# Output items of a pair of batches in neighbouring row parities in turn, stored by one transfer with 4 KB rows; U two items behind V

## The chip, the cores and the metric

The kernel runs on one core of a Trainium2 chip. The core's engines work side by side, each with its own instruction stream: TensorE (PE; its weight loads are listed apart as PEld), VectorE (DVE), ScalarE (ACT), GpSimd (POOL), and SyncE (SP), which here only starts transfers. Sixteen transfer engines move data between the chip's memory (HBM) and the on-chip SBUF; TensorE writes its results into PSUM, eight banks of 2 KB in each of 128 partitions. The metric is the device time of one execution in microseconds (us); lower is better.

## The reference

Eight batches, eight heads, 576 positions, head size 64. Four heads attend to a local window of 32 positions, four to positions at a stride of 32. The heads' outputs, side by side, are x (8 x 576 x 512). The second half mixes x in the frequency domain and ends with a rectified product:

```python
scores = np.where(masks[None, :, :, :], scores, -1000000000.0)
attn = np.exp(scores - np.max(scores, axis=-1, keepdims=True))
attn = attn / (np.sum(attn, axis=-1, keepdims=True) + 1e-09)
x = np.matmul(attn, v)                       # then heads side by side: 8 x 576 x 512
X = np.fft.rfft(x, axis=1)                   # the first 64 modes are mixed
Yr = np.einsum('bmd,mde->bme', Xr, w_r) - np.einsum('bmd,mde->bme', Xi, w_i)
Yi = np.einsum('bmd,mde->bme', Xr, w_i) + np.einsum('bmd,mde->bme', Xi, w_r)
y = np.fft.irfft(Y, n=S, axis=1)             # the other modes are zero
u = x + y
return u + np.maximum(u @ w_ch, 0.0)         # 8 x 576 x 512, float32
```

## The kernel before

Most of the time goes to streaming the mode weights w_r and w_i (64 modes of two 512 x 512 matrices, f32 in HBM, f16 in SBUF) through queues that GpSimd starts, while attention, the forward transform and the products of each mode run under them. The spectrum Y (tile YT) grows mode by mode. In the second half of the run most of the inverse transform is folded in early: `renew` adds what the first three groups of sixteen modes give to the tiles v0 (which hold x @ w_ch, kept as "V") and xo (which hold x, kept as "U").

What is left at the end, and what the change is about, is the last group of modes and the output. The output is cut into 18 items (`items`, L973 to L976). An item is a set of batches and a row tile t. For t < 4 an item has two neighbouring batches and 128 of the 576 rows; tiles t and t+1 (t even) hold the even and the odd rows of the same 256 rows, so a partition's row in tile t and its row in tile t+1 are neighbours in HBM. The last two items (t = 4) hold four batches each and the last 64 rows.

Each item passes these steps:

- `v_early` (L987): two 128 x 512 matmuls with the identity put v0 into a PSUM pair (pool "p").
- `u_early` (L992): the same for xo, into a pair of pool "p" (even items) or "u" (odd items).
- `new_rows` (L1001): for each batch one matmul over only 32 partitions adds the last group of modes, to V from the tile zz (spectrum times w_ch) and to U from the tile yy (spectrum). Batch b uses the 32 partitions of group b mod 4. Matmuls over different groups can run in the array at the same time.
- `v_done` (L1013): ScalarE writes relu(V) into the SBUF tile rl.
- `u_done` (L1020): VectorE adds U and rl into an SBUF tile osb, and SyncE starts the store (L1028). Items with t = 4 are stored by four small transfers, from SyncE for even and ScalarE for odd batches (L1031).

PSUM pool "p" has three pairs, "u" one. osb comes from pool "pw", which has five buffers of 8 KB a partition, the same that held weights before. The rows of one item in one batch are 2 KB each in HBM, and neighbours of an item's rows belong to the other parity, so a store of an item moves runs of 2 KB.

The order of the items is: pair 0 and pair 1 of batches in turn for t = 0, then t = 1, and so on to 3; then pairs 2 and 3; then the two last items. The loop (L1065 to L1081) works on V of item k and U of item k-1 in the same turn, in this order on TensorE: v_early(k), u_early(k-1), new_rows of V(k), new_rows of U(k-1). Ahead of it, V of items 0 and 1 and U of item 0 are put into PSUM under the last modes (`late[22]`), and after the last spectrum the rows of V0 and V1, then U0 and U1, are finished. At item 8 the second half of the last spectrum is multiplied with w_ch (`spec_z(3, 1, held)`), because items from there on belong to batches 4 to 7. The kernel fixes the order of each engine's instructions itself; an engine runs them in order and waits on semaphores.

Of the kernel before, what the change touches and what calls it, by code (L numbers as in the profile page):

```python
# [10 lines left out]
FP = mybir.dt.float32  # L11
F16 = mybir.dt.float16
AluOp = mybir.AluOpType
# [5 lines left out]
DM = 512  # L19
# [37 lines left out]
def kernel(  # L57
# [10 lines left out]
    nc = tc.nc  # L68
# [9 lines left out]
    def psum_pools(**bufs):  # L78
        pctx.close()
        pss.clear()  # L80
        for n, c in bufs.items():
            pss[n] = pctx.enter_context(
                tc.tile_pool(name="ps_" + n, bufs=c, space=PSUM)
            )

    def psum(kind, half=False, pair=False):
        if pair:
            return pss[kind].tile([128, 2, 512], FP, tag=kind, name=kind)
        if half:
            return pss[kind].tile([128, 1024], F16, tag=kind, name=kind)  # L90
        return pss[kind].tile([128, 512], FP, tag=kind, name=kind)
# [39 lines left out]
    pw = ctx.enter_context(tc.tile_pool(name="pw", bufs=NWBUF))  # L131
# [118 lines left out]
    def act_copy(out, in_):  # L250
        nc.scalar.activation(out=out, in_=in_, func=ACTF.Copy)  # L251
# [445 lines left out]
    def out_cols(t):  # L697
        if t < 4:
            return ds(256 * (t % 2) + 128 * (t // 2), 128)
        return ds(512, 64)  # L700
# [32 lines left out]
    def spec_z(g, bq, zp):  # L733
        for e in range(4):
            lhs = YS["YT"][:, e, g, ds(8 * bq, 8), :].rearrange("p x m -> p (x m)")
            nc.tensor.matmul(
                zp, lhs, w_chs["n"][:, e, :], start=(e == 0), stop=(e == 3)
            )
# [131 lines left out]
    yys = [ptr.tile([128, DM], F16, name=f"yy{i}") for i in range(B)]  # L870
# [96 lines left out]
    for n, i in enumerate([3, 5, 7] + list(range(8, 21))):  # L967
        b, t = n // 2, n % 2 * 2
# [3 lines left out]

    items = []  # L973
    for P0 in (0, 2):
        items += [((2 * P, 2 * P + 1), t) for t in range(4) for P in (P0, P0 + 1)]
    items += [(range(b, b + 4), 4) for b in (0, 4)]  # L976
    LAST = len(items) - 1
    vps, ups, rls, osbs = {}, {}, {}, {}

    def own(item, kept, half):  # L980
        bs, t = item
        return [kept[b][:, t] for b in bs] if t < 4 else [half[b // 2] for b in bs[::2]]

    def v_early(k):
        vps[k] = psum("p", pair=True)
        for j, r in enumerate(own(items[k], v0s, v0h)):
            nc.tensor.matmul(vps[k][:, j], idn, r, start=True, stop=False)  # L987

    def u_early(k):
        ups[k] = psum(("p", "u")[k % 2], pair=True)  # L990
        for j, r in enumerate(own(items[k], xos, xoh)):
            nc.tensor.matmul(ups[k][:, j], idn, r, start=True, stop=False)  # L992

    def new_rows(k, acc, spectra):
        bs, t = items[k]
        for j, b in enumerate(bs):
            q = ds(32 * (b % 4), 32)
            o, cols = acc[:, j % 2], out_cols(t)
            if t == 4:
                o = acc[ds(64 * (b % 2), 64), j // 2]  # L1000
            nc.tensor.matmul(  # L1001
                o, A3[q, cols], spectra[b // 4][q], start=False, stop=True
            )

    def pieces(k):
        return [slice(0, 1), slice(1, 2)] if k == 0 else [slice(0, 2)]

    def v_done(k):
        rl = ptr.tile([128, 2, 576], FP, tag=("xT", "rl")[k // 2 % 2], bufs=2, name="rl")
        rls[k] = rl[:, :, 0:DM]  # L1010
        vp = vps.pop(k)
        for j in pieces(k):
            nc.scalar.activation(out=rls[k][:, j], in_=vp[:, j], func=ACTF.Relu)  # L1013

    def u_done(k):
        bs, t = items[k]
        up, rl = ups.pop(k), rls.pop(k)
        osb = pw.tile([128, 2, DM], FP, tag="w", name="osb")
        for j in pieces(k):
            nc.vector.tensor_tensor(  # L1020
                out=osb[:, j], in0=up[:, j], in1=rl[:, j], op=AluOp.add
            )
            if t < 4:
                rows = out[:, ds(128 * (t - t % 2), 256), :].rearrange(
                    "b (p i) e -> p b i e", i=2
                )
                own_b = slice(bs[0] + j.start, bs[0] + j.stop)
                nc.sync.dma_start(rows[:, own_b, t % 2], osb[:, j])  # L1028
        if t == 4:
            for b in bs:  # L1030
                (nc.scalar if b % 2 else nc.sync).dma_start(  # L1031
                    out[b, ds(512, 64), :], osb[ds(64 * (b % 2), 64), b // 2 % 2, :]
                )
# [23 lines left out]
        new_rows(k, vps[k], zzs)  # L1057
    for k in range(2):
        v_done(k)
    for k in range(2):  # L1060
        if k:
            u_early(k)
        new_rows(k, ups[k], yys)
        u_done(k)
    for k in range(2, LAST + 2):  # L1065
        if k == 8:
            held = psum("p", pair=True)[:, 0]
            spec_z(3, 1, held)
            act_copy(zzs[1], held)
        if k <= LAST:  # L1070
            v_early(k)
        if k > 2:
            u_early(k - 1)
        if k <= LAST:
            new_rows(k, vps[k], zzs)
        if k > 2:
            new_rows(k - 1, ups[k - 1], yys)
        if k <= LAST:
            v_done(k)
        if k > 2:  # L1080
            u_done(k - 1)  # L1081
    psum_pools()


# [28 lines left out]
```

## Time and profile before

Device time, median of three runs: 427.61 us (427.32 to 427.89). The profiled execution has a span of 426.7 us from the first to the last instruction; the profile gives that span as its time, and the medians include 0.9 us more around it.

| what | value |
|---|---|
| span of the profiled execution | 426.7 us |
| median of three runs | 427.61 us |
| last weights used, spectrum complete | about 393.3 us |
| first and last add into osb start | 396.16 and 420.06 us |
| one add, 128 x 1024 | 1.225 us |
| one relu, 128 x 1024 | 1.02 us |
| stores by SyncE of 512 KB, issue to landing | 3.4 us median |
| start of one store's issue on SyncE | 0.37 us |
| mean granted TensorE clock | 0.926 |

How to read it: times are from the start of the span. A line of a timeline or a chain gives the start, the duration, the engine, the source line, the operation, the tile written and the tiles read. "SPq" and "ACTq" are instructions that these engines' sequencers run, such as starting a transfer. Landing is when the whole transfer has been signalled as done.

### The profile page before, as it was taken

What the parts mean: (1) busy time and instruction counts of PE and PEld (TensorE: products, weight loads), DVE (VectorE), ACT (ScalarE), POOL (GpSimd) and SP (SyncE); (2) the same over time, 40 slices, a digit from 0 to 9 for tenths busy, and PEclk for the clock granted to TensorE, in tenths of its full rate; (3) what the DMA queues carried; (4) which work ended last, traced back from release to release, by engine and by line L of the source; (5) the groups of instructions that cost most, each with busy time, mean ns of one, the idle gap of its engine ahead of it and who ended that gap; (6) DMA issues with size and microseconds to landing.
All of it is one profiled execution on the core that took longest, in us unless ns stands there. A gap on an engine that the chain in (4) does not pass through costs nothing.

```text
span 426.7 us, 9768 instructions
## 1 busy us (share of the span) xinstructions
PE 346.4 (81%) x4167; PEld 208.2 (49%) x4167; DVE 234.7 (55%) x466; ACT 218.3 (51%) x390; POOL 110.7 (26%) x196
## 2 busy tenths in 40 slices
PE   2977878769999698889768788878788867889993
PEld 2866767554656365566433344435444423445330
DVE  3788778851355154356113246746676354655884
ACT  1687678643656356556642235423442444443872
POOL 8332333322423222222222322222232222210000
PEclk9999899967999689999995889989999979989997
DMA  8999999999999999999999999999999999995698
GB/s 150 210 212 212 213 213 213 211 211 211 214 213 213 213 213 215 212 214 215 210 214 211 213 214 213 210 213 215 212 213 214 213 213 214 214 212 105 244 355 287
DMA packets 30938, 91.62 MB, mean 215 GB/s; under 512 B 4464, under 2 KB 5232, under 8 KB 30896
## 3 DMA queue, kind: packets, MB, share of 16 engines
q0 software_dynamic: 25168, 81.28, 96.2%
q1 hardware_dynamic: 4976, 9.13, 5.9%
q10 hardware_dynamic: 752, 0.61, 0.5%
q8 instruction: 32, 0.52, 0.5%
q14 instruction: 10, 0.08, 0.0%
HBM read 162.83 MB, written 9.44 MB: 404 GB/s over the span
## 4 chain that ended last, share of the span: by engine, by line
DMA 47%; PE 29%; DVE 14%; ACT 5%; issue 3%; DVEq 0%; POOL 0%; ACTq 0%; POOLq 0%
DMA wt<-in_moe_w_i_dram 38%; DMA wt<-in_moe_w_r_dram 7%; PE y L597 5%; DVE xb L241 3%; DVE kz L283 3%; PE p L987 2%; ACT X L251 2%; PE sc L532 2%; PE tp L413 2%; PE sc L459 1%; PE p L1001 1%; PE y L532 1%; PE p L760 1%; DVE yy L752 1%; DVE rec L240 1%
## 5 line engine op out<-in xcount | busy, mean ns | idle before, releaser
L597 PE MATMUL y<-wt,X 128*32 128x512 f16 (+1 forms) x448 | 70.9, 430 | 20.1 <-DMA wt<-in_moe_w_i_dram 20.1
L186 POOL DMA_DIRECT2D wt<-in_moe_w_r_dram x59 | 34.7, 588 | 126.4 <-PE y L597 56.3
L186 POOL DMA_DIRECT2D wt<-in_moe_w_i_dram x60 | 35.4, 590 | 68.3 <-DMA wt<-in_moe_w_i_dram 44.4
L597 PEld LDWEIGHTS <-X 128*32 128x32 f16 (+1 forms) x448 | 28.1, 140 | 39.4 <-DMA wt<-in_moe_w_i_dram 18.6
L727 DVE COPY xo<-tp 128x512 f16<-128x512 f16 x32 | 22.1, 691 | 36.8 <-PE tp L725 36.8
L726 ACT ACTIVATE v<-sc 128x512 f16<-128x512 f32 x32 | 19.1, 597 | 44.2 <-PE sc L717 44.2
L717 PE MATMUL sc<-w_cp,xT 128*128 128x512 f16 x128 | 36.9, 410 | 1.9 <-DVE xT L690 1.9
L489 ACT ACTIVATE PL<-sc 128x480 f16<-128x480 f32 (+1 forms) x48 | 27.0, 578 | 21.3 <-PE sc L475 21.0
L241 DVE TENSOR_TENSOR xb<-av,rec 90x256 f16<-90x256 f32 (+2 forms) x80 | 36.0, 450 | 2.8
L240 DVE RECIPROCAL rec<-av 90x4 f32<-90x4 f32 (+2 forms) x80 | 14.6, 183 | 39.3 <-PE av L504 28.2
L251 ACT ACTIVATE yr<-y 128x512 f16<-128x512 f32 x28 | 16.7, 597 | 36.8 <-PE y L597 35.6
L961 DVE TENSOR_TENSOR xo<-p,xo 128x1024 f16<-128x1024 f32 x16 | 19.6, 1225 | 21.7 <-PE p L760 21.7
L420 DVE COPY qT<-tp 128x576 f16<-128x576 f16 x16 | 11.9, 752 | 34.7 <-PE tp L413 34.7
L251 ACT ACTIVATE v<-p 128x1024 f16<-128x1024 f32 x16 | 16.4, 1023 | 23.1 <-PE p L760 23.1
L378 ACT ACTIVATE PL<-sc 90x360 f16<-90x360 f32 (+1 forms) x48 | 22.7, 490 | 7.0 <-PE sc L371 6.4
L251 ACT ACTIVATE v<-tp 128x640 f16<-128x640 f16 (+1 forms) x24 | 19.0, 807 | 11.8 <-PE tp L447 9.3
L413 PE MATMUL tp<-cI_s,ring 64*64 64x64 f16 x864 | 22.4, 197 | 2.7 <-DVE qT L420 2.4
L459 PE MATMUL sc<-cMl_s,cI_s 128*128 128x480 f16 (+1 forms) x48 | 19.4, 405 | 4.5 <-ACT PL L489 2.9
L276 PE MATMUL tp<-cI_s,ring 72*128 72x72 f16 x256 | 15.4, 207 | 8.7 <-DMA ring<-in_v_dram 7.1
L413 PEld LDWEIGHTS <-ring 64*64 64x64 f16 x864 | 17.5, 110 | 9.4 <-issue 5.4
L251 ACT ACTIVATE kz<-tp 64x360 f16<-64x360 f16 (+1 forms) x32 | 18.9, 592 | 6.2 <-PE tp L413 5.2
L1013 ACT ACTIVATE rl<-p 128x1024 f32<-128x1024 f32 (+1 forms) x19 | 18.4, 979 | 5.7 <-PE p L1001 3.1
(142 smaller groups left out, 737.9 us busy)
## 6 DMA issues: line engine op xcount, KB each, us to landing
wt<-in_moe_w_i_dram POOLq DMA_DIRECT2D x60, 512.0 KB, 18.8
wt<-in_moe_w_r_dram POOLq DMA_DIRECT2D x59, 512.0 KB, 17.7
out_dram<-osb SPq DMA_DIRECT2D x15, 512.0 KB, 3.4
ring<-in_v_dram POOLq DMA_DIRECT2D x8, 288.0 KB, 13.4
ring<-in_q_dram POOLq DMA_DIRECT2D x8, 288.0 KB, 13.6
ring<-in_k_dram POOLq DMA_DIRECT2D x8, 288.0 KB, 13.1
ring<-in_v_dram POOLq DMA_DIRECT2D x3, 512.0 KB, 14.8
ring<-in_q_dram POOLq DMA_DIRECT2D x3, 512.0 KB, 14.8
```

The costliest lines, as they stand in the source:

```text
L186: nc.gpsimd.dma_start(dst, rows)
L241: nc.vector.tensor_tensor(out=dst, in0=val.rearrange("p h (q c) -> p h c q", c=4), in1=rec[0:n, 0:pieces] .to_broadcast((n, pieces, 64)) . ...
L251: nc.scalar.activation(out=out, in_=in_, func=ACTF.Copy)
L378: nc.scalar.activation(out=PS[0:n, ds(POFF[t], 4 * n)], in_=scp[0:n, 0 : 4 * n], func=ACTF.Exp, scale=SCALE,)
L413: nc.tensor.transpose(tp[ds(64 * hp, 64), ds(64 * i, 64)], qn[ds(64 * hp, 64), ds(64 * (9 * g + i), 64)], idn[ds(64 * hp, 64), ds(64 * hp, ...
L459: nc.tensor.matmul(scp[:, 0 : n * times].rearrange("p (h x) -> p h x", h=times), idn, mask_rows("cMl", n, times), start=True, stop=False,)
L489: nc.scalar.activation(out=dst, in_=src, func=ACTF.Exp, scale=SCALE)
L597: nc.tensor.matmul(yp[ds(a, 32), :], Xh[half][pr, c].rearrange("p b r (h m) -> p (b r h) m", h=2)[:, :, mm % 32], wt[pr, XC[c], :], start= ...
L717: nc.tensor.matmul(vp, xT[:, ch], w_chs["cp"][:, ch, :], start=(ch == 0), stop=(ch == 3),)
L726: nc.scalar.activation(out=v0, in_=vp, func=ACTF.Copy)
L727: nc.vector.tensor_copy(out=xo.rearrange("p (h q c) -> p h q c", h=2, c=4), in_=tp[:, 0:512].rearrange("p (h c q) -> p h q c", h=2, c=4),)
L961: nc.vector.tensor_tensor(out=xo, in0=up[:, 0:n], in1=xo, op=AluOp.add)
```

## The change

Four things change together. The order of the items: for each pair of batches, tiles t and t+1 now come directly after each other, then the same for the other pair. One osb buffer holds two items, the two parities side by side, so that a partition's two rows are 4 KB in one piece both in SBUF and in HBM. The store is started after the second item of such a pair, and moves 1 MB in rows of 4 KB; items 0 and 1 are still stored apart, item 0 in two pieces. The lag of U behind V (`LAG`) is two items instead of one, and the first two U items are drawn into the loop. The last two items (t = 4) and their stores stay as they are.

```diff
     for P0 in (0, 2):
-        items += [((2 * P, 2 * P + 1), t) for t in range(4) for P in (P0, P0 + 1)]
+        items += [
+            ((2 * P, 2 * P + 1), t + i)
+            for t in (0, 2)
+            for P in (P0, P0 + 1)
+            for i in range(2)
+        ]
     items += [(range(b, b + 4), 4) for b in (0, 4)]
...
+    LAG = 2
...
-        osb = pw.tile([128, 2, DM], FP, tag="w", name="osb")
+        if t == 4:
+            osb = pw.tile([128, 2, DM], FP, tag="w", name="osb")
+        elif t % 2 == 0:
+            osbs[k] = osbs[k + 1] = pw.tile([128, 2, 2, DM], FP, tag="w", name="osb")
         for j in pieces(k):
-            nc.vector.tensor_tensor(
-                out=osb[:, j], in0=up[:, j], in1=rl[:, j], op=AluOp.add
-            )
-            if t < 4:
-                rows = out[:, ds(128 * (t - t % 2), 256), :].rearrange(
-                    "b (p i) e -> p b i e", i=2
-                )
-                own_b = slice(bs[0] + j.start, bs[0] + j.stop)
-                nc.sync.dma_start(rows[:, own_b, t % 2], osb[:, j])
+            to = osb[:, j] if t == 4 else osbs[k][:, j, t % 2]
+            nc.vector.tensor_tensor(out=to, in0=up[:, j], in1=rl[:, j], op=AluOp.add)
+            if t == 4 or (k > 1 and t % 2 == 0):
+                continue
+            i = slice(t % 2, t % 2 + 1) if k < 2 else slice(0, 2)
+            rows = out[:, ds(128 * (t - t % 2), 256), :].rearrange(
+                "b (p i) e -> p b i e", i=2
+            )
+            own_b = slice(bs[0] + j.start, bs[0] + j.stop)
+            nc.sync.dma_start(rows[:, own_b, i], osbs[k][:, j, i])
...
-    for k in range(2):
-        if k:
-            u_early(k)
-        new_rows(k, ups[k], yys)
-        u_done(k)
-    for k in range(2, LAST + 2):
+    for k in range(LAST + 1 + LAG):
+        u = k - LAG
         if k == 8:
             held = psum("p", pair=True)[:, 0]
             spec_z(3, 1, held)
             act_copy(zzs[1], held)
-        if k <= LAST:
+        if 2 <= k <= LAST:
             v_early(k)
-        if k > 2:
-            u_early(k - 1)
-        if k <= LAST:
+        if u > 0:
+            u_early(u)
+        if 2 <= k <= LAST:
             new_rows(k, vps[k], zzs)
-        if k > 2:
-            new_rows(k - 1, ups[k - 1], yys)
-        if k <= LAST:
+        if u >= 0:
+            new_rows(u, ups[u], yys)
+        if 2 <= k <= LAST:
             v_done(k)
-        if k > 2:
-            u_done(k - 1)
+        if u >= 0:
+            u_done(u)
```

## The prediction

> **What bounds the kernel now.** I read the page first, then the rows of the last 30 us in order of time, then short windows of the transfer engines and SyncE's waits. The changed code runs only after the mode matmuls, so everything before about 395 us stays as it is. The page:
>
> ```profile
> span 426.7 us, 9768 instructions
> PE 346.4 (81%) x4167; PEld 208.2 (49%) x4167; DVE 234.7 (55%) x466; ACT 218.3 (51%) x390; POOL 110.7 (26%) x196
> GB/s 150 210 212 212 213 213 213 211 211 211 214 213 213 213 213 215 212 214 215 210 214 211 213 214 213 210 213 215 212 213 214 213 213 214 214 212 105 244 355 287
> ```
>
> Each slice is 10.7 us. Up to 384 us the weights stream in at 212 GB/s (as f16; the f32 side is twice that, 424 GB/s) and bound the kernel. The dip to 105 is the pause between the last weight and the first store; the last two slices are the stores. The store stage on VectorE, in order of time (start, duration, line, tiles, shape; in brackets the idle time before it and what ended that):
>
> ```profile
> 396.16 1.29 DVE L1020 TENSOR_TENSOR osb<-p,rl 128x512 f32<-128x512 f32 x2 [0.55 <-ACT rl L1013]
> 397.56 1.23 DVE L1020 TENSOR_TENSOR osb<-u,rl 128x1024 f32<-128x1024 f32 x1
> 399.07 1.22 DVE L1020 TENSOR_TENSOR osb<-p,rl 128x1024 f32<-128x1024 f32 x1 [0.28 <-PE p L1001]
> 400.37 1.23 DVE L1020 TENSOR_TENSOR osb<-u,rl 128x1024 f32<-128x1024 f32 x1
> ...
> 417.39 1.23 DVE L1020 TENSOR_TENSOR osb<-u,rl 128x1024 f32<-128x1024 f32 x1 [0.37 <-PE u L1001]
> 418.92 1.23 DVE L1020 TENSOR_TENSOR osb<-p,rl 128x1024 f32<-128x1024 f32 x1 [0.31 <-PE p L1001]
> 420.06 1.22 DVE L1020 TENSOR_TENSOR osb<-u,rl 128x1024 f32<-128x1024 f32 x1
> ```
>
> One add an item, every 1.295 us, of which 1.225 is the add. The chain of waits gives the same period to TensorE, one turn of the loop:
>
> ```profile
> 399.47 0.43 PE u L992 x2
> 399.90 0.32 PE p L1001 x2
> 400.23 0.54 PE p L987 x2
> 400.77 0.43 PE p L992 x2
> ```
>
> 0.54 (V early) + 0.43 (U early) + 0.32 (new rows of both) = 1.29. So the loop is bound by TensorE with VectorE only 0.07 us behind. A third resource is as full; the transfer engines by windows (columns: us, busy of PE, PEld, DVE, ACT, POOL, granted clock, share, GB/s):
>
> ```profile
> 409.00:420.00 11.00, 10.69 (x72) 3.23 (x68) 9.89 (x9) 8.19 (x8) 0.00 (x0) 1.00 1.02 379
> 421.00:422.00 1.00, 0.00 (x0) 0.00 (x0) 0.28 (x1) 0.00 (x0) 0.00 (x0) 0.96 0.94 244
> 422.00:425.10 3.10, 0.00 (x0) 0.00 (x0) 0.00 (x0) 0.00 (x0) 0.00 (x0) 0.50 0.86 297
> ```
>
> From 409 to 420 us they are busy all the time at 379 GB/s, while the adds make 0.524 MB each 1.295 us, 405 GB/s. A backlog builds: the store issued at 407.97 landed 2.8 us later, that of 417.05 landed 3.5 us later, so 7 stores landed in 9.78 us, 1.40 us each. After the last add (421.28) the queue drains until 425.05, and the program closes at 426.7. The last landing is the wait that ends last:
>
> ```profile
> SPq L1108 <- DMA out_dram<-osb: 2.7, 3, 1.5
> out_dram<-osb SPq DMA_DIRECT2D x4, 128.0 KB, 2.8
> out_dram<-osb ACTq DMA_DIRECT2D x4, 128.0 KB, 3.3
> ```
>
> **The change part by part.** All sums are against this execution's span of 426.7; the median, 427.61, lies 0.9 above it, and I carry a difference over unchanged.
>
> *Order of items.* The same 18 items, matmuls, relus and adds. TensorE's 0.32 us for four new-row matmuls needs four different 32-row groups. With a lag of two, V of item k and U of item k-2 always belong to the two different pairs of batches, as k and k-1 do now; so the period stays 1.295. V of items 0 and 1 now share row groups, about 0.2 us (one 512-column pass, the 0.43 of two halved), covered by the relus of item 0: V of item 2 starts only when both are done (396.67 now), so nothing. Without that cover the 0.2 would count.
>
> *The lag, on the path.* U of items 0 and 1 no longer fills the wait for those relus (add at 396.16) but rides in the turns of items 2 and 3. V of item k keeps its time; U of item k has the time that U of item k+1 has now. At the end one turn is added that holds a U alone. U of item 15 comes in V17's turn: its add, by the spacing of the last long turn (1.63 us of TensorE after 417.39, minus little), starts near 419.0 and ends 420.2; items 16 and 17 follow on VectorE at 1.225 + 0.07: last add from 421.4 to 422.65. That is 1.36 us later than 421.28. At the block for the second half of the spectrum (404 to 406 us) the accumulator buffers rotate differently: V of item 8 gets one freed by an old add instead of the relu that ended 405.18; TensorE's four matmuls there end at 405.09 and V began 405.23, so at most 0.1 is won. The relu's buffer waits for the add of four items earlier, now two turns back instead of three; 1.3 us of slack remain: nothing.
>
> *The adds* write the same 1,024 elements with a step; same row, 1.225. Bounds: 1.225, or worse by the 0.07 of slack before the period moves; taken at nothing.
>
> *Stores.* SyncE issues 7 transfers of 1 MB in place of 14 of 512 KB: 7 issues of 0.37 us fewer, all beside waiting, nothing. Each pair is sent when its second item is done, so the first waits one turn more; osb buffers are fewer but hold two items, and five of them cover ten items: no wait. A 1 MB transfer with 4 KB rows has no row in the trace. Upper bound: two of today's stores, 2.78 us. Lower bound: the rate at which these engines took the weights' larger pieces, 1.049 MB at 424 GB/s, 2.47 us. I take 2.6, nearer the middle, since production is one pair per 2.59 us and the backlog then stands still. This gains 0.2 a pair, but only in the queue; it shortens nothing as long as the adds come later.
>
> *The tail, which decides.* The store of items 14 and 15 is issued at 420.22; from issue to first packet takes 0.87 (first store: issued 396.88, engines start 397.75): 421.09. It needs 2.6: 423.7. Behind and between it come the 8 small stores of items 16 and 17, unchanged, 1.05 MB in 2 KB rows: at the saturated 385 GB/s 2.72 us, at the drain's present 297 GB/s 3.53 us. I take 3.0, nearer the full rate, because a backlog stands in front of them now. 421.09 + 2.6 + 3.0 = 426.7 against 425.05: **+1.65**; bounds 421.09 + 2.47 + 2.72 = 426.28 (+1.2) and 421.09 + 2.78 + 3.53 = 427.4 (+2.35).
>
> *The added wait.* In the built program the last small store on SyncE (batch 6) takes over the completion semaphore of the 1 MB store, so SyncE holds it until that has landed: 421.09 + 2.6 + 0.35 (half of the ScalarE queue's first stores between) + 0.5 (last packet to landing, 425.05 to 425.58) = 424.5. Then 2.1 (first store) to 2.8 us (small ones now): 426.6 to 427.3 against 425.58, +1.0 to +1.7. Nothing but the end is queued behind it. Both paths agree, and I take +1.6 (0.05 off for item 8): **429.2**.
>
> A rule against the trace. The row: back-to-back 512 KB stores land every 1.40 us, and a single one in 2.8 to 3.5. The Trainium skill, page "DMA: Bandwidth & Descriptors", section Bandwidth, says to batch transfers to 1 MiB or more, and its section on the anatomy of one DMA fits a transfer as 2.0 us plus bytes at 436 GB/s: 3.2 us for 512 KB (agrees), an estimated 4.4 us for 1 MB. Paid one after the other, merging would save 2 us a pair, 14 in all, and this kernel would be at 413; the landings show the fixed part overlapped, so the saving is 0.2 a pair at most. The same fit speaks against the change at the end, as the last big store would land near 424.6.
>
> **The rivals.** *A: the drain absorbs the shift (not slower).* Place: 421 to 425 us. For it: the last small store is issued at 422.32, 3.3 us before its landing, where an unloaded one took 2.1; with no backlog, the end would be 422.65 + 0.1 + 0.6 (second issue of the queue) + 2.1 = 425.45 against 425.58, and with SyncE's held store some 0.5 more: about 427.5 to 428.1. It decides if the last 2.1 MB are through 4.8 us after 421.09 (0.85 later than now), 437 GB/s; against it: 393 is the best microsecond of the stores. *B: the held store costs more.* The 1 MB store shares with ScalarE's queue and lands near 425.2; then 2.8 more, 428.0, +2.4: 430.0. For it: one of the small stores' issues took 0.85 us. *C: the period falls.* If the 0.11 us that V early takes more than U early were a wait that the lag removes, TensorE's period would be 1.18; 16 turns times 0.115 is 1.84, less 1.65: 427.4. It decides below 1.19 a turn. Against it: the add alone takes 1.225. *D: the rows are cut to 2 KB anyway*: stores at 2.78 a pair, +0.18: 429.4.
>
> **How the numbers follow.** Forecast 0.70, A 0.10, B 0.12, C 0.05, D 0.03. About 0.2%, 0.86 us, is what a measurement can tell from no change. Forecast, B and D are slower: 0.85. A is within: 0.10, and C is split: faster 0.03, within 0.02. Range: forecast bounds +1.0 to +2.35, stretched to +0.7 towards A and +2.5 to take in B: 428.3 to 430.1; left out are A, C and the edges, under 0.2.
>
> **What would show it.** Right: first add near 397.7, period still 1.29, last add starting near 421.4; 4 KB packets, about half as many in the stores' queue; the engines full until 424 and done near 426.7; the last SyncE issue near 424.5, apart from the others. Wrong: a last add before 421; a period off 1.29 (four new-row matmuls over 0.32); adds waiting for a store; the last landing under 426.2 (A) or over 427.6 (B).

## The result and the profile after

The changed kernel takes 429.67 us (median of four runs, 429.43 to 430.45) against 427.64 us before (median of four): a ratio of 1.0045, 95% interval 1.0032 to 1.0059. It is 2.0 us slower. The prediction was 429.2 with a range of 428.3 to 430.1.

The two profiled spans differ by only half of that. The page after:

```profile
span 427.7 us, 9754 instructions
GB/s 149 213 213 213 213 213 212 212 210 212 214 213 213 213 213 214 213 215 213 211 213 210 214 214 213 212 213 215 213 213 213 213 213 214 214 211 84 231 370 282
q1 hardware_dynamic: 3072, 9.13, 5.6%
```

427.7 against 426.7 us. The rest is in where the stage of stores begins. The last write of the spectrum (YT) by VectorE closes the part that the change doesn't touch. It ended at 393.27 us in the execution profiled before (start 392.98) and at 392.29 in this one:

```profile
392.00 0.29 DVE L563 TENSOR_TENSOR YT<-y,Y 128x128 f16<-128x128 f32 x1 [2.95 <-PE y L630]
393.87 0.76 DVE L1063 COPY yy<-yp 128x512 f16<-128x512 f16 x2 [1.58 <-PE yp L1061]
396.73 1.29 DVE L1030 TENSOR_TENSOR osb<-p,rl 128x512 f32<-128x512 f32 x2 [2.11 <-PE p L1007]
398.08 1.23 DVE L1030 TENSOR_TENSOR osb<-u,rl 128x1024 f32<-128x1024 f32 x1
399.38 1.23 DVE L1030 TENSOR_TENSOR osb<-p,rl 128x1024 f32<-128x1024 f32 x1
...
417.74 1.23 DVE L1030 TENSOR_TENSOR osb<-u,rl 128x1024 f32<-128x1024 f32 x1 [0.42 <-PE u L1007]
418.88 1.22 DVE L1030 TENSOR_TENSOR osb<-p,rl 128x1024 f32<-128x1024 f32 x1
420.06 1.23 DVE L1030 TENSOR_TENSOR osb<-u,rl 128x1024 f32<-128x1024 f32 x1
```

The weights' arrival varies by about a microsecond from execution to execution, so from here on every time is counted from the end of that last write of YT. The whole stage, to the end of the span, took 33.40 us before and takes 35.43 us now: +2.03, the same as the medians. (My sum took the execution profiled before as lying 0.9 us below the median. Each run after lists span and time together, 427.71 and 429.49 for the profiled one, so some 1.8 us lie around a span, and the execution profiled before was itself about 0.8 us slower than the median.)

The adds show the first half of the loss: the first starts 1.57 us later (4.45 after the spectrum, not 2.88), the period is still 1.30, and the last ends 1.00 later (29.00, not 28.00).

The second half is in the transfers. Windows of the transfer engines, first from the first to the last packet of the stage, then from the end of the last add to the last packet, and three short ones (columns: us, busy of PE, PEld, DVE, ACT, POOL, granted clock, share of the transfer engines, GB/s). Before:

```profile
397.74:425.05 27.31, 21.80 (x136) 6.78 (x134) 20.55 (x17) 16.80 (x17) 0.00 (x0) 0.94 0.95 346
421.27:425.05 3.78, 0.00 (x0) 0.00 (x0) 0.01 (x1) 0.00 (x0) 0.00 (x0) 0.59 0.88 283
```

After:

```profile
398.33:426.09 27.76, 21.10 (x131) 6.64 (x129) 20.44 (x17) 15.54 (x16) 0.00 (x0) 0.94 0.89 341
421.29:426.09 4.80, 0.00 (x0) 0.00 (x0) 0.00 (x0) 0.00 (x0) 0.00 (x0) 0.63 0.96 316
401.71:402.84 1.13, 1.13 (x12) 0.41 (x8) 1.07 (x2) 0.97 (x1) 0.00 (x0) 1.00 0.07 29
408.15:408.88 0.73, 0.73 (x8) 0.19 (x5) 0.73 (x1) 0.73 (x1) 0.00 (x0) 1.00 0.02 6
419.39:419.89 0.50, 0.50 (x6) 0.11 (x4) 0.50 (x1) 0.00 (x0) 0.00 (x0) 1.00 0.04 16
```

Share times length gives the busy time: 25.9 of 27.31 us before, 24.7 of 27.76 after. The 4 KB rows save 1.2 us of transfer time, but the engines stand still for 3.1 us in place of 1.4. In the three short windows they move next to nothing: all that may be sent has been sent, and the next pair's store was issued late, because it had to wait for its second item. The issues on SyncE that ended the three gaps:

```profile
401.94 0.38 SPq L1038 DMA_DIRECT2D out_dram<-osb  x1
407.99 0.37 SPq L1038 DMA_DIRECT2D out_dram<-osb  x1
418.99 0.37 SPq L1038 DMA_DIRECT2D out_dram<-osb  x1
```

Each is 0.9 us ahead of the first packet that ends the gap (402.84, 408.88, 419.89). Most of the first gap and all of the other two lie in these 0.9 us. To leave no gap, the pair's second item would have had to be done 0.9 us before the engines run out of the stores in front. From the last add to the last packet it now takes 4.80 us, not 3.78. The stores at the end, by size (KB each, median us to landing):

```profile
out_dram<-osb SPq DMA_DIRECT2D x1, 1024.0 KB, 4.2
out_dram<-osb SPq DMA_DIRECT2D x4, 128.0 KB, 3.6
out_dram<-osb ACTq DMA_DIRECT2D x4, 128.0 KB, 3.7
```

Of SyncE's waits, the one for a transfer before a small store (us in total, times, longest):

```profile
SPq L1041 <- DMA out_dram<-osb: 0.4, 1, 0.4
```

The last 1 MB lands 4.2 us after its issue, and the small stores land 0.4 to 0.8 us later after their issue than before (2.8 and 3.3). The last SyncE store was held for the 1 MB store, as predicted, but for 0.4 us only.

### The profile page after: what moved, and what is told of

Same layout as the page of the kernel before. It is cut to its first block, busy times and chain, and to the rows that moved or that the text cites. A ratio compares the mean times of both kernels' runs of the same rounds, so it can differ in the third digit from the quotient of the medians.

```text
span 427.7 us, 9754 instructions
## 1 busy us (share of the span) xinstructions
PE 344.5 (81%) x4167; PEld 207.3 (48%) x4167; DVE 234.9 (55%) x466; ACT 218.3 (51%) x390; POOL 110.8 (26%) x196
## 3 DMA queue, kind: packets, MB, share of 16 engines
q1 hardware_dynamic: 3072, 9.13, 5.6%
## 4 chain that ended last, share of the span: by engine, by line
DMA 56%; PE 22%; DVE 12%; ACT 4%; issue 3%; POOL 1%; DVEq 0%; POOLq 0%; ACTq 0%
DMA wt<-in_moe_w_i_dram 40%; DMA wt<-in_moe_w_r_dram 10%; DMA ring<-in_v_dram 4%; PE y L597 3%; DVE xb L241 3%; DVE kz L283 2%; PE p L993 2%; PE sc L532 2%; ACT X L251 2%; DMA ring<-in_q_dram 1%; PE p L1007 1%; DVE yy L752 1%; DVE rec L240 1%; PE sc L717 1%; PE av L392 1%
## 5 line engine op out<-in xcount | busy, mean ns | idle before, releaser
L597 PE MATMUL y<-wt,X 128*32 128x512 f16 (+1 forms) x448 | 68.9, 420 | 20.9 <-DMA wt<-in_moe_w_i_dram 20.9
```

The source lines that it names most:

```text
L597: nc.tensor.matmul(yp[ds(a, 32), :], Xh[half][pr, c].rearrange("p b r (h m) -> p (b r h) m", h=2)[:, :, mm % 32], wt[pr, XC[c], :], start= ...
```

## The experiments

The theory after the result: the lag of two costs 1.0 us, because the last U comes later, and storing in pairs costs 1.0 us more in the transfers. Rival 1: the lag is all. Rival 2: the merged stores are all. The table gives each run's median ratio to the kernel before, and from its profile, counted from the spectrum, the end of the last add, the last packet, and the difference of the two ("drain").

| run | ratio (95%) | last add | last packet | drain |
|---|---|---|---|---|
| before | 1 | 28.00 | 31.78 | 3.78 |
| after | 1.0045 (1.0032 to 1.0059) | 29.00 | 33.80 | 4.80 |
| e1, last pair apart | 1.0035 (1.0021 to 1.0048) | 29.00 | 33.59 | 4.59 |
| e2, lag two, no merging | 1.0027 (1.0016 to 1.0037) | 28.99 | 32.95 | 3.96 |
| e3, merging, lag one | 1.0064 (1.0050 to 1.0078) | 29.63 | 34.35 | 4.72 |
| e4, lag two in the old order | 1.0090 (1.0074 to 1.0106) | 31.85 | 35.67 | 3.82 |
| e5, merging in the old order | 1.0049 (1.0034 to 1.0065) | 28.00 | 34.07 | 6.07 |
| e6, small stores by two | 1.0011 (1.0003 to 1.0019) | 28.00 | 32.45 | 4.45 |
| e7, last rows early | 1.0041 (1.0025 to 1.0058) | 28.50 | 33.71 | 5.21 |
| e8, four stores left out | 0.9998 (0.9987 to 1.0009) | 28.01 | 31.91 | 3.90 |
| e9, two stores by GpSimd | 1.0054 (1.0041 to 1.0066) | 28.00 | 32.53 | 4.53 |
| e10, item 16 not stored | 0.9993 (0.9983 to 1.0003) | 28.00 | 31.34 | 3.34 |
| e11, two stores a pair | 1.0022 (1.0013 to 1.0031) | 28.99 | 32.97 | 3.98 |
| e12, the same, both late | 1.0044 (1.0030 to 1.0058) | 28.99 | 34.20 | 5.21 |

### The lag and the merging apart (e2, e1)

```diff
# e2, against the changed kernel
-            if t == 4 or (k > 1 and t % 2 == 0):
+            if t == 4:
                 continue
-            i = slice(t % 2, t % 2 + 1) if k < 2 else slice(0, 2)
+            i = slice(t % 2, t % 2 + 1)
```

> The changed kernel with its order and its lag of two, but every item stored by itself as before, 512 KB in 2 KB rows. Theory: only the added turn of U is left, +1.0: 428.6 us; the transfers of 2 KB rows take 85 ns each and land every 1.4 us, so that a backlog is back and perhaps 0.3 is lost again (428.9). Rival 1 (the lag is all): 429.6. Rival 2 (the merge is all): 427.7.

Measured: 429.08 us, ratio 1.0027, 0.2 above the theory's upper figure and 0.5 below rival 1's. The stage shows it more sharply: last add 28.99 as in the changed kernel, and a drain of 3.96, near that of the kernel before. The windows of this run, laid as above:

```profile
398.45:425.36 26.91, 21.11 (x131) 6.65 (x129) 20.44 (x17) 15.56 (x16) 0.00 (x0) 0.95 0.96 351
421.40:425.36 3.96, 0.00 (x0) 0.00 (x0) 0.00 (x1) 0.00 (x0) 0.00 (x0) 0.64 0.86 279
```

With single stores the engines are busy 96% of the stretch though the adds are as late as in the changed kernel; the stage closes at 34.40, 1.00 after the kernel before. So by the stage the lag alone costs 1.0 us and merging 1.0 us more. By the medians, each against the kernel before in its own session, e2 is 1.29 us slower and e11 below, which sends its stores at the same times, 0.94; the split is known to some 0.3 us. Both rivals fall.

```diff
# e1, against the changed kernel
-            if t == 4 or (k > 1 and t % 2 == 0):
+            if t == 4 or (2 <= k < 14 and t % 2 == 0):
                 continue
-            i = slice(t % 2, t % 2 + 1) if k < 2 else slice(0, 2)
+            i = slice(0, 2) if 2 <= k < 14 else slice(t % 2, t % 2 + 1)
```

> The changed kernel, but items 14 and 15 (the last pair before the small stores) are stored apart, 512 KB each in 2 KB rows, item 14 as soon as it is added. Theory: the change cost 2.0 us, about 1.0 because U's last turn was added and about 1.0 because half of the last 1 MB store could have gone 1.3 us earlier. It expects the second part back: 428.6 us, last add unchanged, last landing about 4.3 us after the last add ends as in the kernel before. Rival 1 (the lag is all, the drain only follows): 429.6, no change. Rival 2 (the merged store and the last SyncE store held behind it are all): 427.7.

Measured: 429.55 us, 1.76 above the kernel before where the change is 2.03 above; the last packet comes only 0.2 us earlier (33.59). This part of the theory was wrong: the last pair's late first half makes up at most 0.3 of the second microsecond. By then the queue is already behind: item 15's store, issued 26.7 us after the spectrum in e1 and in e2, lands 3.7 us after its issue in e1 and 3.0 in e2. The first two gaps stand in e1 as in the changed kernel, and the third, before the last pair, is gone.

### Is it the row groups that ask for the lag? (e3, e4)

```diff
# e3, against the changed kernel
-    LAG = 2
+    LAG = 1
# e4, against the kernel before: its items and stores, the changed kernel's loop
+    LAG = 2
...
+    for k in range(LAST + 1 + LAG):
+        u = k - LAG
```

> The changed kernel with the lag set back to one. Every second turn now has V and U of the same pair of batches, which use the same 32-row groups of TensorE: two passes in place of one, 0.54 in place of 0.32 us, 8 turns, +1.76; the added U turn is gone. Theory: +1.7 for the turns and +1.0 for the last 1 MB store: 430.3 us, and turns that alternate between 1.3 and 1.5 us. Rival 1 (the lag is all of the loss and merging costs nothing): 429.4. If sharing row groups costs nothing: theory 428.6, rival 1 427.6.

> The kernel before (its order of items and its stores) with the lag of two alone. V of item k and U of item k-2 are always of the same pair of batches, so every full turn costs 0.22 us more: 14 turns, +3.1, and the added turn of U +1.0: 431.7 us, period 1.51. If sharing row groups costs nothing, 428.6 and a period of 1.295. Rival 2 (the merge is all of the loss, the lag costs nothing): 430.7 with sharing, 427.6 without.

Measured: e3 430.74, e4 431.64 us. The chain of waits in e4, one turn:

```profile
408.33 0.43 PE u L993 x2
408.76 0.32 PE p L1002 x2
409.08 0.22 PE u L1002 x2
409.30 0.54 PE p L988 x2
```

0.32 has become 0.32 + 0.22, a period of 1.51, and 3.85 us at the last add. In e3 the turns alternate between 1.35 and 1.46, 2.81 a pair in place of 2.59, and the last add ends 1.63 later than before. So sharing the 32-row groups costs 0.22 us a turn; of the two lags tried with the order that puts a pair's two parities next to each other, two items is the cheaper at the last add (1.00 later, against 1.63).

### Deferral or the transfers themselves? (e5, e11, e12)

```diff
# e5, against the kernel before: items 4 to 11
-        osb = pw.tile([128, 2, DM], FP, tag="w", name="osb")
+        if t == 4 or not 4 <= k < 12:
+            osb = pw.tile([128, 2, DM], FP, tag="w", name="osb")
+        elif t % 2 == 0:
+            osbs[k] = osbs[k + 2] = pw.tile([128, 2, 2, DM], FP, tag="w", name="osb")
...
+            if 4 <= k < 12 and t % 2 == 0:
+                continue
...
+                nc.sync.dma_start(rows[:, own_b], osbs[k][:, j])
```

> The kernel before with its order and its lag of one, but items 4 to 11 stored in pairs (4 with 6, 5 with 7, 8 with 10, 9 with 11), 1 MB each in rows of 4 KB; the first four and the last six items and their stores are untouched. New theory: the end is set by the transfer queue's own sum, first packet plus busy time plus idle time; merging saves 0.6 us of busy time (4 KB packets took 164 ns where two of 2 KB take 170 to 178), but the queue runs dry while a pair waits for its second item, about 2 us in the middle of the stage. It expects +1.3 us, 429.0, with the last add unchanged. Rival (only the last stores and the time of the last add count): 427.5, at best 0.3 faster.

Measured: 430.39 us (+2.3). The adds are those of the kernel before, to the last one at 28.00, and the last six items and their stores are untouched; still the last packet is 2.3 us late. The windows of the whole stretch and of its two large gaps, which end 0.9 us after the issue of a pair that waited for its second item:

```profile
397.27:426.87 29.60, 21.80 (x136) 6.79 (x134) 20.54 (x17) 16.79 (x17) 0.00 (x0) 0.94 0.86 319
403.98:405.94 1.96, 1.82 (x11) 0.58 (x9) 1.03 (x1) 1.26 (x2) 0.00 (x0) 1.00 0.05 18
411.22:412.29 1.07, 1.07 (x12) 0.41 (x8) 1.00 (x2) 0.97 (x1) 0.00 (x0) 1.00 0.04 15
```

And the last ordinary store, that of item 15, in the list of issues:

```profile
out_dram<-osb SPq DMA_DIRECT2D x1, 512.0 KB, 5.5
```

The store of item 15 lands 5.5 us after its issue, 3.2 in the kernel before. The size was off (by the shares 4.1 us idle in place of 1.4, 2.7 more and not 2), but the rival, that only the last stores count, is excluded: bytes held back early come out at the end, because the engines run near their limit afterwards (379 GB/s, with 405 coming from the adds) and can't make up for it. At the very end another thing adds to it: SyncE's small stores were held 2.6 us in all by waits for landings, and the last of them landed last. Item 15's landing lies ahead of that, and it is 2.26 us later than in the kernel before (30.86 against 28.60 after the spectrum).

```diff
# e11, against the changed kernel; e12 has slice(1, 2) first
-            nc.sync.dma_start(rows[:, own_b, i], osbs[k][:, j, i])
+            for i1 in (i,) if k < 2 else (slice(0, 1), slice(1, 2)):
+                nc.sync.dma_start(rows[:, own_b, i1], osbs[k][:, j, i1])
```

> The changed kernel with the same order, lag and moment of storing, but each pair is stored by two transfers of 512 KB with 2 KB rows, issued one after the other when the second item is done. It takes the 4 KB rows alone away. Theory (the queue's sum sets the end of the changed kernel, and the 4 KB rows save 1.0 us of busy time, 24.6 in place of 25.6): +0.9 us against the changed kernel, 430.5. Rival (the rows' length saves nothing, all that counts is when the last stores start): 429.6.

Measured: 428.80 us. The run didn't do what it was to do. SyncE's first transfer of a pair waits only for the add of the first item, and it was issued right after that, at the same times as in e2. So it measures the lag alone a second time, and agrees with e2 in the stage (32.97 and 32.95).

> The changed kernel with the same order and lag, each pair stored when its second item is done, but by two transfers of 512 KB with 2 KB rows, the second item's half first, so that SyncE cannot send the first item's half early (in the run before this one it did, which made that run a second look at the lag alone). It takes the 4 KB rows away and keeps the deferral. Theory (the loss beside the lag comes from the deferral, by which the queue runs dry; 4 KB rows give a part back): no faster than the changed kernel, 429.7 to 430.5, with gaps in the transfers at the same places as there. Rival (the 1 MB transfers or their 4 KB rows are what costs, not the deferral): as with the lag alone, 428.8.

Measured: 429.99 us, ratio 1.0044, the same as the changed kernel within the interval, and not 428.8. With both halves late and rows of 2 KB:

```profile
398.75:426.91 28.16, 21.11 (x131) 6.65 (x129) 20.44 (x17) 15.55 (x16) 0.00 (x0) 0.96 0.92 336
402.13:403.26 1.13, 1.13 (x12) 0.41 (x8) 1.07 (x2) 0.96 (x1) 0.00 (x0) 1.00 0.07 27
```

The gap of 1.13 us is the same as in the changed kernel; the second is 0.43 us long in place of 0.73, and the third is gone. Between e2 and e12 only the moment at which the first halves are sent differs, and the order of the two halves. It is worth 1.25 us at the last packet (32.95 to 34.20), and against the kernel before e12 is 1.99 us slower by its median, e2 1.29 and e11 0.94 (the intervals of e11 and e12 just touch). With e5, which shows the same in the old order, that makes the deferral the cause.

Between e12 and the changed kernel the rows and the number of transfers differ: 0.4 us at the last packet in favour of the 4 KB rows (34.20 to 33.80). A part of it isn't the rows. In e12 SyncE was held longer before its last small store, 0.9 us in place of 0.4:

```profile
SPq L1042 <- DMA out_dram<-osb: 0.9, 1, 0.9
```

That store was the last to land, 0.26 us after the last of ScalarE's. The device times don't differ (1.99 and 2.03 above the kernel before). So the deferral costs, and it isn't shown that the 4 KB rows give a part of it back at the end: they save 1.2 us of transfer time against e12 (24.7 for 25.9), and the engines stand still for 3.1 us in place of 2.3.

### What sets the end of the kernel before? (e8, e10, e6, e7, e9)

These looked for the price of the backlog and of the small stores, and for a version faster than both.

```diff
# e8
-                nc.sync.dma_start(rows[:, own_b, t % 2], osb[:, j])
+                if not 8 <= k < 12:
+                    nc.sync.dma_start(rows[:, own_b, t % 2], osb[:, j])
# e10
-            for b in bs:
+            for b in bs if k > 16 else ():
# e9
-                (nc.scalar if b % 2 else nc.sync).dma_start(
+                (nc.gpsimd if b in (1, 2) else nc.scalar if b % 2 else nc.sync).dma_start(
# e6; e7 has nc.sync twice, and the two items at places 8 and 13
-            for b in bs:
-                (nc.scalar if b % 2 else nc.sync).dma_start(
-                    out[b, ds(512, 64), :], osb[ds(64 * (b % 2), 64), b // 2 % 2, :]
-                )
+            for h, eng in enumerate((nc.sync, nc.scalar)):
+                eng.dma_start(
+                    out[bs[0] + h : bs[0] + 4 : 2, ds(512, 64), :].rearrange(
+                        "j p e -> p j e"
+                    ),
+                    osb[ds(64 * h, 64)],
+                )
```

> The kernel before with the stores of items 8 to 11 left out (2 MB of the output are not written); all adds are kept. It shows what a queue without backlog would be worth. Theory: the backlog at the last items is 0.7 us and goes: -0.7, 427.0, with the drain after the last add 3.6 in place of 4.3 us. Rival (the drain after the last add is made of the small stores alone): no change, 427.7.

Measured: 428.15 us, ratio 0.9998. The engines stood still for 5 us in the middle, and the end is where it was:

```profile
409.73:414.77 5.04, 5.04 (x36) 1.64 (x32) 4.75 (x5) 4.03 (x4) 0.00 (x0) 1.00 0.00 0
420.70:424.60 3.90, 0.00 (x0) 0.00 (x0) 0.00 (x1) 0.00 (x0) 0.00 (x0) 0.72 0.85 269
```

The backlog of the kernel before costs nothing that this run resolves. Its drain of 3.8 us belongs to the last items' small stores. The reading that fits all runs with the old small stores is that there are two limits, and the later one sets the end: the last add plus 3.8 to 4.0 us for the small stores (before, e2, e4, e8, e11), or the queue's own sum of first packet, busy time and gaps, which exceeds it in every run that holds stores back (after, e1, e3, e5, e12). This is a reading and no test of its own: first packet, busy time and gaps add up to the last packet in every run, so what separates the two cases is the length of the gaps.

> The kernel before without the stores of the first of the two last items (512 KB of the output are not written); all adds are kept. It bounds what the small stores cost: the last item's four stores can be issued at 421.3 and 421.9, with the queue done with all else by 421.4. Theory (a small store lands 2.1 to 2.8 us after its issue when nothing is in front): last landing at 30.8 after the spectrum is complete in place of 32.3, -1.3 us. Rival (the last landing hangs on the last add alone): no change, 32.3.

Measured: 427.55 us, a drain of 3.34, so the last packet 0.44 us earlier and the last landing 0.63 (31.67 for 32.30), not 1.3. Most of the drain is the last item's own four stores, issued two by two behind each other; why they need over 3 us is left open.

> The kernel before, but the last two items are stored by two transfers of 256 KB each (one from SyncE, one from ScalarE) in place of four of 128 KB. The eight small stores take 0.42 us each where 0.34 is the saturated rate. Theory (the queue's sum, and some of it lost between small transfers): the 0.5 us that are neither busy nor idle shrink to 0.2, -0.3 us: 427.4. Rival (the issues of four small stores a queue, 0.6 us each, set the end): -1.0, 426.7.

Measured: 428.64 us, slower by 0.1%, both expectations missed. Half as many transfers of twice the size took 0.67 us longer.

> The kernel before with the two items of the last 64 rows moved from the end to places 8 and 13, stored by SyncE in two transfers of 256 KB each; the block for the second half of the spectrum comes at item 9. The last two items are ordinary ones. Theory (the queue's sum): the same bytes with the same first packet; without the small transfers at the end 0.5 us are saved and the idle time stays: 427.2, about 0.4 faster, last add about as before. Rival (the end is the last add plus the issues and landings of the small stores): last add plus 3.3 instead of 4.3 us, -1.0: 426.7.

Measured: 429.77 us, slower. The last add ends 0.5 later, and SyncE's issues behind the 256 KB transfers take up to 1.5 us, so that the queue falls behind; the ordinary stores at the end land 5.1 us after their issue.

> The kernel before, but of the first of the two last items the stores of batches 1 and 2 are issued by GpSimd, so that SyncE and ScalarE issue three small stores each in place of four. If the chain of small issues sets the end of the kernel before (new theory, after the run without backlog ended no sooner), the last issue comes 0.4 us earlier, at 421.9 in its scale, and the end 0.4 earlier: 427.3 against 427.7. Rival (the end is set by the packets of the small stores, whoever issues them): no change. A loss is possible if GpSimd's stores start more than 1 us later than SyncE's.

Measured: 430.19 us, slower. The last issue did come 0.5 us earlier, but the last packet 0.75 later, and the span closes 2.8 us after the last landing in place of 1.1. None of these beats the kernel before; it remains the fastest.

## Why the prediction was right

The direction, the size (+1.6 against +2.0) and the range held. By its steps:

- *Order of items*: the period was to stay 1.295, and the row groups of V and U were to stay apart. Right: 1.30 with the change, and 1.51 where the groups are shared (e4).
- *The lag, on the path*: first add near 397.7 in the scale of the execution before, that is 4.4 after the spectrum; it came 4.45 after. The last add was to end 1.36 later; it ended 1.00 later. The mis-sized term is the block at item 8, put at 0.1 at most: the adds on its two sides start 2.15 us apart, not 2.46, so it gave 0.3.
- *The adds*: right, 1.225 with the new step.
- *Stores, a 1 MB store at 2.6 us*: right for the transfer itself where one pair follows another. The 4 KB packets took 164 ns each in the trace, 16 of them on each engine 2.6 us. Wrong in what followed: "production is one pair per 2.59 us and the backlog then stands still" took it that there is a backlog. There was none when the pairs began, and the engines stood still while they waited for second items. The step that I costed as a small gain in the queue is a loss: 1.25 us at the last packet from e2 to e12, and the 1.2 us of transfer time that the longer rows save mostly turned into waiting.
- *The tail*: the last large store was to start at 421.09 (27.82 after the spectrum), take 2.6 and be followed by 3.0 for the small ones. Its first packet came at 27.60, its last 4 KB packet ended 2.94 later, and the small ones ended 3.26 after that, at 33.80; predicted 33.43. The reason given, "because a backlog stands in front of them now", did not justify putting the small stores near the full rate: from 422.83, the end of the last 4 KB packet, to 426.09 the engines moved 300 GB/s, not 385, at a busy share of 0.94. The sum rests on the lateness of the last pair alone. e1 shows that this was only part of the matter: without that lateness the gaps of the earlier pairs make the queue nearly as late (33.59). So the size came out near for a mechanism that the prediction had only in part, and partly by luck: the last large store started 0.2 us earlier than summed, since the lag cost less, and it and the small stores took 0.6 longer.
- *The added wait*: SyncE was held as said, but for 0.4 us, and the last landing is that of a ScalarE store which was not held. So this path, which the prediction counted as agreeing with its sum, didn't set the end of the changed kernel. In e5 and e12, where the waits were longer, the last landing is that of the held store.
- *The rule against the trace*: saving 14 us was excluded rightly. The first and the last 1 MB stores, each behind a gap, landed after 4.0 and 4.2 us. The fit in the Trainium skill, page "DMA: Bandwidth & Descriptors", section "Anatomy of one DMA — SWDGE (gpsimd) path", gives an estimated 4.4; the page states it for transfers that GpSimd issues, and these are issued by SyncE.

Rival A (the drain absorbs the shift) fell: the drain grew. So did B, C and D: the held wait was short, the period stayed, the packets were 4 KB (3,072 packets in SyncE's queue, 4,976 before).

## What to carry to other kernels

Where stores run near the transfer engines' limit, count the time at which each byte may start, not only the rate. A store that waits for a second item let the engines run dry here, and a stage that produces about as fast as they can take gave little of it back, even when it happened in the middle (e5: 2.7 us more idle time, 2.3 us later). Longer rows paid nothing here because they held bytes back. When two parts of a loop are shifted against each other by one more turn, look for that turn at the end: here it was 1.0 us.

## What the hardware did that I had not expected

- A small store's issue took longer in the runs that hold stores back: the second ones took 1.24 (SyncE) and 1.26 us (ScalarE) in the changed kernel and up to 1.6 in e5, 0.58 and 0.85 before. In e12, with transfers of 512 KB in front, they took 1.29 and 1.35, so the 1 MB size is not what it takes.
- ScalarE's first small store was issued at 420.13 in the changed kernel, and the first packet of its queue started at 422.95, after the last 4 KB packet of SyncE's queue had ended (422.83). It did not run between them, as I had assumed.
- Transfers from 64 partitions got slower when two of 128 KB were made into one of 256 KB (e6): 176 and 207 GB/s in the two microseconds from 28 to 30 after the spectrum, where the kernel before moved 244 and 322.
- Two stores by GpSimd added 1.7 us between the last landing and the end of the span (e9).
